# Other places for eight token tiles and eight modulation rows in the first pass of an attention and mixer kernel

## The chip, the cores and the metric

One core of a Trainium2 chip runs the whole kernel. The metric is the device time of one execution in microseconds (us); a kernel's time is the median of several executions. The engines are PE (TensorE matmul; PEld are its weight loads), DVE (VectorE), ACT (ScalarE), POOL (GpSimd) and SP (SyncE), whose queue issues the transfers.

## What is computed

A block with modulated layer norms: infini-attention with a compressive memory (32 heads of width 32, 4 segments of 512 tokens), then a token-mixing MLP. All tensors are float32.

```python
mod = (silu(c) @ w_mod).reshape(1, 6, 1, -1)
sa, ca, ga, sb, cb, gb = (mod[:, i] for i in range(6))
h = layernorm(x) * (1 + ca) + sa               # x: 1 x 2048 x 1024
x = x + ga * A(h)                              # A: attention, below
h = layernorm(x) * (1 + cb) + sb
x = x + gb * B(h)                              # B: gelu(W1 h^T) W2 over the tokens

# A, for segment s in 0..3 of each head; M and z start at 0
p = softmax(qs @ ks.T * scale + causal mask)
o = g * (phi(qs) @ M) / (phi(qs) @ z + 1e-6) + (1 - g) * (p @ vs)
M, z = M + phi(ks).T @ vs, z + sum(phi(ks))
```

The projections are h @ wq, h @ wk, h @ wv, and the outputs of all heads go through wo.

## The kernel before

**Precision.** Most matmuls run on operands that are split into a high part (rounded to the matmul's format) and a low part (the rest): three matmuls high x high, high x low and low x high stand for one. The helper split (L117) makes such a pair: a cast on one engine (L121 on ACT or L123) and a subtraction on another (L124). That is done for weights, for the normalised tokens and for the scores' operands.

**Two passes.** The attention works on 16 iterations t in each of two passes (its, L364): pass 0 treats segments 0 and 1 for the eight groups of four heads, pass 1 segments 2 and 3. Pass 0 converts each group's weights: fetch_part (L150) loads 128 x 1024 of them into a buffer "raw", split_part (L155) makes two pairs of it (two casts L121 on ACT, two subtractions L124 on DVE), and keep_w (L172) stores the pairs in DRAM (wsp), from where pass 1 loads them. There are three parts for each group.

**The loop.** The loop at L690 goes over steps n from -3. Step n issues the scores of head n (scores, L512: matmuls a, three exponentials on ACT, a cast L532 on ACT and two subtractions L534 on POOL), the row maxima of head n + 3 (maxima, L473: matmuls sx, sy, sz into two PSUM banks, each taken by DVE at L485), the values of head n - 1 (values, L536) and a piece of the projections of head n + 8 (project, L380: matmuls nps at L194, kps, qps at L202, and the transfers sk at L376 to L378 that lay out the operands of the next heads). A step number thus counts heads; head n belongs to iteration n // 4.

**Work planned into steps.** plan (L594) hangs a function on a step, later (L662) a fetch on one step and its use on another. The functions of a step are issued at its end (L715). With "V", "A" or "G" each instruction of the function on that engine is queued behind a mark of the same step (behind, L504): the last row maximum on DVE, which in step n is that of head n + 3 (L485), the cast of head n on ACT (L532), or its subtraction on POOL (L534). Apart from that an instruction goes into its engine's queue at the place that the builder's schedule gives it, from the order of issue and from when its inputs and buffers are free. Each engine then works through its queue in order; so does SP with its transfers.

**Token tiles.** Segments 2 and 3 are tokens 1024 to 2047, eight tiles of 128. load_gaw (L668) loads one tile of x into gaw, a single buffer. token_tile (L254) normalises it in place (statistics L129 to L137 and L240 on DVE with two small ACT steps, then L241 on ACT), transposes it in eight blocks on PE into PSUM (L262), applies the modulation on the way back (eight ACT steps at L265), casts the high part into a raw buffer (L268 on ACT), subtracts for the low part (two POOL steps at L270), and stores both in DRAM (hT1, L273). reload_h (L359) brings them back for pass 1. Before, tile i is loaded in step 6i and treated in step 6i + 3.

**Late modulation.** The rows 2048 to 6143 of the transposed w_mod are needed late. mod_fetch (L571) loads 128 of them into a raw buffer, mod_late (L576) multiplies them by the activated c and sums each row on DVE (L577). After row 7 and after row 31 mod_rows (L584) transposes the sums and stores them. Row j is fetched in step 36 + 2j, for j from 8 on in step 44 + 2j, and summed one step later.

**The buffers raw.** There are three. The weight parts, the high parts of the token tiles, the modulation rows and later the parts of wo share them, in program order.

**The plan of the weights.** Group g (2 to 7) starts at n = 8g - 13: parts are fetched in steps n, n + 1 and n + 2 and converted in n + 1, n + 3 and n + 4. That gives conversions in steps 4, 6, 7, then 12, 14, 15, then 20, 22, 23, and so on to 44, 46, 47.

Of the kernel before, what the change touches and what calls it, by code (L numbers as in the profile page):

```python
# [31 lines left out]
VL = 1  # L32
PHB = 2
P32B = 2
ML0 = 36
HB = 3
WO0 = 65
WOS = 6
# [5 lines left out]
def attention_and_mlp(ctx, tc, x, wq, wkv, wo, beta, w1, b1, w2, b2, c, wm_a, wm_b, out):  # L44
    nc = tc.nc
    V, A, G, T, SY = nc.vector, nc.scalar, nc.gpsimd, nc.tensor, nc.sync
# [27 lines left out]
    def bank(tag, bufs, name):  # L74
        return psum.tile([P, 512], F32, tag=tag, bufs=bufs, name=name)
# [162 lines left out]
    def norm_x(pool, t):  # L238
        mv = ln_stats(pool, t, "a")
        V.tensor_scalar(mv[:, 3:4], mv[:, 0:1], -1.0, mv[:, 2:3], op0=ALU.mult, op1=ALU.mult)  # L240
        A.activation(t, t, AF.Identity, scale=mv[:, 2:3], bias=mv[:, 3:4])  # L241
# [12 lines left out]
    def token_tile(tt):  # L254

        r = gaw
        norm_x(a, r)
        for half in range(2):
            ps = bank("s2", 2, f"hpl{tt}_{half}")
            for i in range(4):  # L260
                ct = 4 * half + i
                T.transpose(ps[:, 128 * i:128 * i + 128], r[:, P * ct:P * ct + P], ident)  # L262
            for i in range(4):
                ct = 4 * half + i
                A.activation(r[:, P * ct:P * ct + P], ps[:, 128 * i:128 * i + 128], AF.Identity,  # L265
                             scale=saca[:, ct, 1:2], bias=saca[:, ct, 0:1])
        hi = a.tile([P, D], F32, tag="raw", bufs=3, name=f"hix{tt}")
        A.copy(hi.bitcast(F32R), r)  # L268
        for c in (slice(0, 512), slice(512, 1024)):
            G.tensor_tensor(r[:, c].bitcast(F32R), r[:, c], hi[:, c], op=ALU.subtract)  # L270
        i = tt % 4
        for part, t in enumerate((hi, r)):
            SY.dma_start(hT1[tt // 4 - 2, :, :, part, P * i:P * i + P].rearrange("k p n -> p k n"),  # L273
                         t.rearrange("p (k n) -> p k n", k=NK))
# [296 lines left out]
    def mod_fetch(j):  # L571
        r = a.tile([P, D], F32, tag="raw", bufs=3, name=f"rawm{j}")
        SY.dma_start(r, wm_b[P * j:P * j + P])
        return r

    def mod_late(j, r):  # L576
        V.scalar_tensor_tensor(r, r, 1.0, scb, op0=ALU.mult, op1=ALU.mult, accum_out=mcol[:, j:j + 1])  # L577
        if j == 7:
            mod_rows(0, 8)
        if j == 31:  # L580
            V.tensor_scalar_add(mcol[:, 16:24], mcol[:, 16:24], 1.0)
            mod_rows(8, 32)
# [11 lines left out]
    def plan(n, f, engines=""):  # L594
        todo.setdefault(n, []).append((f, engines))
# [66 lines left out]
    def later(n, fetch, m, f, engines):  # L662

        got = []
        plan(n, lambda: got.append(fetch()))
        plan(m, lambda: f(got[0]), engines)

    def load_gaw(i):  # L668
        with tc.issue_after(last_sk[0, 3].ins):
            return SY.dma_start(gaw, x[P * (8 + i):P * (9 + i)])  # L670

    for i in range(8):
        later(6 * i, lambda i=i: load_gaw(i),
              6 * i + 3, lambda r, i=i: token_tile(8 + i), "V")
    for g in range(2, NG):
        n = 8 * g - 13
        plan(n, lambda g=g: W.__setitem__((0, g), {}))
# [2 lines left out]
                  n + n1, lambda r, g=g, kind=kind, part=part: split_part(g, kind, part, r), "A")  # L680
        plan(n + 4, lambda g=g: keep_w(g))
    for j in range(32):
        n = ML0 + 2 * j + (8 if j >= 8 else 0)
        later(n, lambda j=j: mod_fetch(j), n + 1, lambda r, j=j: mod_late(j, r), "V")
    plan(WO0 - 3, lambda: spread(gaw, 0))
    for i in range(8):
        n = WO0 + WOS * i
        later(n, lambda i=i: wo_fetch(i), n + 1, lambda r, i=i: wo_split(i, r), "G")

    for n in range(-LEADS, 4 * NI + VL):  # L690
# [18 lines left out]
        if 4 * NI - 5 <= m < 4 * NI + 3:  # L709
            i = m - 4 * NI + 5  # L710
# [434 lines left out]
```

## Time and profile before

| | us |
|---|---|
| median of 3 executions | 2233.55 (2232.91 to 2235.92) |
| profiled execution | 2234.21 |
| its span, first to last instruction | 2231.4 |
| mean granted clock of PE | 0.995 |
| DVE busy in the span | 1675.0 |
| ACT busy in the span | 1137.5 |

How to read the rows. The profile is one execution. L194 is line 194 of the kernel. "nps<-wv,h" names the tile written and the tiles read. In a timeline row stand the start, the duration, engine, line, operation, tiles and count, and in brackets the idle time of the engine just before it and what ended that. In a row of groups stand the busy time and the mean ns of one after the bar, then the idle time before them with its releasers. In the rows of one tile's instructions stand the shortest, the median and the longest duration in ns, and the first and the last start. "SPq" is the issue of a transfer, not the transfer. A busy PE is not a PE at its peak: the granted clock says at what share of full speed its clock ran.

### The profile page before, as it was taken

How to read it: one execution, taken by the hardware profiler on the slowest of the kernel's cores; microseconds unless marked ns; L12 is line 12 of the kernel's file. 1: busy time of each engine (PE TensorE's matmuls, PEld its weight loads, DVE VectorE, ACT ScalarE, POOL GpSimd, SP SyncE). 2: the span in 40 equal slices, each digit the busy share in tenths (PEclk: the TensorE clock that was granted, in tenths of full speed). 3: DMA queues.
4: the chain of work that ended last, by engine and by line, in shares of the span. 5: the costliest groups of instructions: out<-in, count | busy, mean ns of one | idle time of the engine just before them, and what ended most of it. 6: DMA issues, size and time to landing. Idle time of an engine off the chain costs nothing.

```text
span 2231.4 us, 38273 instructions
## 1 busy us (share of the span) xinstructions
PE 2195.2 (98%) x13786; PEld 1886.7 (85%) x13786; DVE 1675.0 (75%) x3762; ACT 1137.5 (51%) x2082; POOL 725.4 (33%) x831
## 2 busy tenths in 40 slices
PE   8999999999999999999999999999999999999999
PEld 5989898889989999988888888888888888888887
DVE  7677676767776776765858766888888886969687
ACT  5477776667666666654636533533334242424232
POOL 2175665656766766653001200033330000000000
PEclk9999999999999999999999999999999999999999
DMA  7657565688556666764654587655556542414134
GB/s 284 190 168 210 161 186 156 186 287 245 158 178 192 189 192 202 216 217 151 217 198 177 222 314 268 245 221 221 206 204 224 208 142 63 150 57 146 57 123 151
DMA packets 175185, 423.05 MB, mean 190 GB/s; under 512 B 17524, under 2 KB 71828, under 8 KB 166036
## 3 DMA queue, kind: packets, MB, share of 16 engines
q1 hardware_dynamic: 174996, 420.61, 57.2%
q8 instruction: 109, 1.79, 0.3%
q14 instruction: 80, 0.66, 0.1%
HBM read 244.62 MB, written 125.06 MB: 166 GB/s over the span
## 4 chain that ended last, share of the span: by engine, by line
PE 87%; DVE 4%; POOL 3%; DMA 3%; ACT 3%; issue 1%; SPq 1%; ACTq 0%; POOLq 0%; DVEq 0%
PE mx L925 47%; PE nps L194 12%; PE po L795 7%; PE qps L202 7%; PE pv L548 3%; POOL ph L534 2%; PE a L519 1%; PE sz L483 1%; PE sx L483 1%; DMA rawm<-in_wm_b_dram 1%; PE a L522 1%; PE rd L455 1%; PE sy L483 1%; PE up L465 1%; PE srow L296 1%
## 5 line engine op out<-in xcount | busy, mean ns | idle before, releaser
L925 PE MATMUL mx<-bU,sp 128*128 128x512 f32 x2352 | 534.4, 389 | 1.0 <-DVE ac L932 0.9
L925 PEld LDWEIGHTS mx<-bU,sp 128*128 128x128 f32 x2352 | 441.3, 188 | 93.6 <-issue 1.3
L121 ACT CAST sp<-wr 128x384 fp32r<-128x384 f32 (+2 forms) x408 | 217.2, 545 | 432.6 <-PE mx L925 351.9
L534 POOL TENSOR_TENSOR ph<-p,ph 128x640 f16<-128x640 f32 x256 | 384.9, 1524 | 161.2 <-ACT ph L532 156.9
L194 PE MATMUL nps<-wv,h 128*128 128x256 f32 x3072 | 435.2, 282 | 1.7 <-DVE h L124 0.7
L925 PE MATMUL mx<-bA,sp 128*128 128x512 f32 x1764 | 430.5, 389 | 0.0
L194 PEld LDWEIGHTS nps<-wv,h 128*128 128x128 f32 x3072 | 403.4, 189 | 9.7 <-DVE h L124 2.0
L925 PEld LDWEIGHTS mx<-bA,sp 128*128 128x128 f32 x1764 | 331.2, 188 | 68.7
L124 DVE TENSOR_TENSOR sp<-wr,sp 128x384 fp32r<-128x384 f32 (+2 forms) x408 | 259.7, 647 | 25.4 <-ACT sp L121 25.2
L932 DVE TENSOR_TENSOR ac<-mx,ac 128x512 f32<-128x512 f32 x280 | 189.9, 687 | 85.9 <-PE mx L925 85.5
L202 PE MATMUL qps<-h,wq 128*128 128x512 f32 x768 | 197.2, 400 | 0.4
L532 ACT CAST ph<-p 128x1280 f16<-128x1280 f32 x128 | 161.0, 1259 | 39.5 <-POOL p L530 39.1
L795 PE MATMUL po<-wo,ots 128*128 128x512 f32 x768 | 180.0, 390 | 0.0
L795 PEld LDWEIGHTS po<-wo,ots 128*128 128x128 f32 x768 | 143.5, 188 | 28.9
L202 PEld LDWEIGHTS qps<-h,wq 128*128 128x128 f32 x768 | 142.0, 191 | 28.7 <-ACT vp L406 1.2
L925 PE MATMUL mx<-bB,sp 128*128 128x512 f32 x588 | 164.0, 389 | 0.0
L530 POOL TENSOR_SCALAR_AFFINE_SELECT p<-p 128x256 f32<-128x256 f32 x256 | 123.1, 491 | 91.8 <-ACT p L527 50.9
L548 PE MATMUL pv<-vp,ph 128*128 128x97 bf16 (+1 forms) x2560 | 142.7, 202 | 0.7 <-DVE red L555 0.4
L548 PEld LDWEIGHTS <-ph 128*128 128x128 f16 x2560 | 115.8, 98 | 21.8 <-issue 9.3
L925 PEld LDWEIGHTS mx<-bB,sp 128*128 128x128 f32 x588 | 110.4, 188 | 22.9
L485 DVE CUSTOM_DVE_ANT_0 sx<-sx,mask 128x128 f32<-128x128 f32 (+1 forms) x256 | 93.8, 366 | 47.5 <-PE sx L483 45.2
L932 DVE TENSOR_TENSOR cc<-mx,cc 128x512 f32<-128x512 f32 x140 | 94.9, 684 | 36.7 <-PE mx L925 36.7
(207 smaller groups left out, 3146.6 us busy)
## 6 DMA issues: line engine op xcount, KB each, us to landing
sk<-sg SPq DMA_DIRECT2D x384, 128.0 KB
wr<-in_w_dram SPq DMA_DIRECT2D x28, 1024.0 KB
wr<-in_w_dram SPq DMA_DIRECT2D x32, 768.0 KB
bstu<-ucd SPq DMA_DIRECT2D x28, 768.0 KB
wsp<-wv SPq DMA_DIRECT2D x32, 512.0 KB
rawm<-in_wm_b_dram SPq DMA_DIRECT2D x32, 512.0 KB
wv<-wsp SPq DMA_DIRECT2D x32, 512.0 KB
pcd<-cc SPq DMA_DIRECT2D x14, 1024.0 KB
```

The costliest lines, as they stand in the source:

```text
L121: last_hi[0] = A.copy(hi, src)
L124: return lo_eng.tensor_tensor(lo, src, hi.bitcast(F32), op=ALU.subtract)
L194: T.matmul(ps[:, aa], h[:, j, 128 * tt:128 * tt + 128], wt[:, i, o:o + 256], start=(n == 0), stop=(n >= 6 * NK - 2), skip_group_check=True)
L202: T.matmul(ps, wt[:, i, o:o + 128], h[:, j], start=(k + n == 0), stop=(3 * k + n == 3 * NK - 1))
L485: marks[4 * t + h - LEADS, "V"] = V.tensor_tensor_reduce(o, o, mask[:, 384 - 128 * i:], 1.0, -3.0e38, op0=ALU.add, op1=ALU.max, accum_out= ...
L530: G.affine_select(w, w, pattern=[[0, 2], [1, 128]], compare_op=ALU.is_ge, fill=0.0, base=0, channel_multiplier=-1)
L532: marks[n, "A"] = A.copy(ph[:, 0], p32)
L534: marks[n, "G"] = G.tensor_tensor(ph[:, 1, c], p32[:, c], ph[:, 0, c], op=ALU.subtract)
L548: T.matmul(pv[:, i, 0:w], ph[:, part, o:o + 128], d["vp"][:, j, h, 0:w], start=(n == 0), stop=(n == 19), skip_group_check=True)
L795: T.matmul(ps, os_[:, i, P * ct:P * ct + P], wop[ct, nh][:, j], start=(n == 0), stop=(n == 3 * NK - 1))
L925: T.matmul(ps, ops[q][:, i, P * k:P * k + P], b[:, j], start=(m == 0 and first), stop=(m == 3 * nk - 1), skip_group_check=True)
L932: V.tensor_tensor(d, ps, d, op=ALU.add)
```

## The change

Token tile i is loaded and treated in other steps, with two steps between load and treatment instead of three: treated in 2, 8, 11, 16, 19, 24, 27 and 32 instead of 3, 9, 15, 21, 27, 33, 39 and 45. The modulation rows 0 to 7 are fetched in steps 33, 34, 40, 41, 42, 48, 49 and 50 instead of 36, 38, 40, 42, 44, 46, 48 and 50, and summed one step after their fetch as before. The rows from 8 on stay in their steps (44 + 2j, written in another way). The weights keep their plan.

```diff
-ML0 = 36
+ML0 = 44
...
-    for i in range(8):
-        later(6 * i, lambda i=i: load_gaw(i),
-              6 * i + 3, lambda r, i=i: token_tile(8 + i), "V")
+    for i, n in enumerate((2, 8, 11, 16, 19, 24, 27, 32)):
+        later(n - 2, lambda i=i: load_gaw(i), n, lambda r, i=i: token_tile(8 + i), "V")
...
     for j in range(32):
-        n = ML0 + 2 * j + (8 if j >= 8 else 0)
+        n = (33, 34, 40, 41, 42, 48, 49, 50)[j] if j < 8 else ML0 + 2 * j
         later(n, lambda j=j: mod_fetch(j), n + 1, lambda r, j=j: mod_late(j, r), "V")
```

## The prediction

> **What bounds the kernel now.** I read the page first, then the busy time of each engine by stretches, then the waits of TensorE (PE), then the timeline at each hole.
>
> ```profile
> span 2231.4 us, 38273 instructions
> PE 2195.2 (98%) x13786; PEld 1886.7 (85%) x13786; DVE 1675.0 (75%) x3762; ACT 1137.5 (51%) x2082; POOL 725.4 (33%) x831
> ```
>
> PE is busy for 98% of the span, so no edit that leaves its work as it is can bring more than the 36.2 us in which it is idle. The stretches below (columns: length, then busy us of PE, PEld, DVE, ACT, POOL, then granted clock, DMA share, GB/s) say where these lie.
>
> ```profile
> 75.00:340.00 265.00, 260.43 (x2241) 238.41 (x2240) 190.67 (x561) 186.90 (x357) 153.19 (x181) 0.97 0.60 173
> 340.00:475.00 135.00, 123.64 (x1050) 112.28 (x1049) 100.11 (x284) 92.59 (x173) 81.49 (x89) 0.97 0.67 197
> 500.00:960.00 460.00, 456.27 (x4104) 419.25 (x4103) 332.54 (x1013) 296.98 (x526) 319.18 (x380) 1.00 0.64 194
> 960.00:2231.00 1271.00, 1266.03 (x5787) 1048.10 (x5785) 985.22 (x1767) 509.72 (x937) 143.84 (x117) 1.00 0.52 183
> PE sz L483 <- DVE mx L485: 8.4, 4, 4.0
> ```
>
> The first pass of the attention runs from about 75 to 475. Its last 135 us lose 11.4 us of PE, the 265 us before them 4.6, and the whole second pass 3.7. The last row is from the waits within 340 to 475: 8.4 of the 11.4 us are four waits of one kind. PE wants to write the next score tile, and the bank is still held because DVE has not taken the row maximum of the one before. DVE is not short of time there (100 of 135 us); it works through its queue in order, and something long stands ahead of the maximum. The timeline says what:
>
> ```profile
> 358.93 0.42 SPq L573 DMA_DIRECT2D rawm<-in_wm_b_dram  x1
> 367.99 1.47 DVE L577 SCALAR_TENSOR_TENSOR rawm<-rawm,scb 128x1024 f32<-128x1024 f32 x1 [5.36 <-DMA rawm<-in_wm_b_dram]
> 370.31 0.79 PE L483 MATMUL sz<-sk 96*128 96x512 f32 x1 [3.99 <-DVE mx L485]
> 392.61 0.95 DVE L124 TENSOR_TENSOR wq<-rawq,wq 128x512 fp32r<-128x512 f32 x1
> 394.40 0.49 PE L483 MATMUL sz<-sk 96*128 96x512 f32 x1 [2.04 <-DVE mx L485]
> 430.11 1.30 DVE L577 SCALAR_TENSOR_TENSOR rawm<-rawm,scb 128x1024 f32<-128x1024 f32 x1
> 432.61 3.21 DVE L124 TENSOR_TENSOR wv<-rawv,wv 128x512 fp32r<-128x512 f32 x2
> 436.65 0.50 PE L483 MATMUL sz<-sk 96*128 96x512 f32 x1 [1.62 <-DVE mx L485]
> ```
>
> At 358.93 the first modulation row is fetched; it lands 9.06 us later, DVE has stood 5.36 us for it, and PE 3.99 us behind DVE. At 394 and 436 the maxima stand behind the second halves of a weight conversion (L124), with token-tile or modulation work of the same queue around it. The clock adds to this:
>
> ```profile
> 365.00:370.00 5.00, 1.32 (x23) 1.02 (x20) 2.01 (x5) 4.38 (x9) 3.56 (x5) 0.92 0.47 114
> 370.00:375.00 5.00, 4.20 (x24) 3.41 (x24) 4.96 (x18) 0.58 (x1) 1.43 (x3) 0.50 0.56 198
> 375.00:380.00 5.00, 5.00 (x23) 4.15 (x21) 2.21 (x3) 3.17 (x5) 2.08 (x2) 0.89 0.83 274
> 245.00:250.00 5.00, 2.46 (x21) 1.79 (x17) 5.00 (x12) 5.00 (x12) 3.91 (x5) 0.98 0.45 182
> 250.00:255.00 5.00, 5.00 (x38) 4.46 (x38) 3.19 (x11) 3.78 (x7) 2.77 (x2) 0.68 0.31 91
> 120.00:125.00 5.00, 4.52 (x38) 3.01 (x34) 4.74 (x20) 5.00 (x11) 2.40 (x5) 0.85 0.32 66
> 125.00:130.00 5.00, 4.84 (x26) 3.71 (x24) 3.43 (x10) 3.24 (x7) 5.00 (x7) 0.50 0.81 239
> 130.00:135.00 5.00, 5.00 (x18) 4.16 (x17) 2.73 (x4) 4.69 (x7) 2.53 (x4) 0.63 1.00 264
> ```
>
> After the hole at 366 the granted clock is 0.50 from 370 to 375 and 0.89 to 380: 5 x 0.50 + 5 x 0.11 = 3.05 us of full-speed work lost. The hole at 245 (2.54 us idle) is followed by 0.68: 1.6 us more. Between 120 and 135, with little idle time but few matmuls, the clock costs 0.75 + 2.5 + 1.85 = 5.1 us. So a stall is dearer than its idle time.
>
> The Trainium skill (TensorE: Matmul & The Clock Gate, What's actually happening) says that the array falls to half rate after an idle window of about 3.4 us and needs a busy one to rise again. By that rule a hole of 4 us is followed by half clock, some 1.7 us a window (an estimate from the page's window), and holes of 1 to 2 us cost their idle time only; the trace agrees at 366 and disagrees at 245 and 120, where the single holes are shorter and the clock falls all the same. By the rule the sum below would be -9.0 instead of -9.6 us, and the slower rival would end at no change, since four meetings at 2.54 us are 10.2 us against credits of 6.2 + 2.45 + 1.62.
>
> **The change, part by part.** No instruction and no transfer is added or removed: eight token tiles and eight modulation rows move, each with all that it issues.
>
> ```profile
> L265 ACT ACTIVATE gaw<-hpl,saca x64: 443/470/519, 119.4 to 448.8; 128x128 f32<-128x128 f32 x64
> L129 DVE BATCH_NORM_STATS2 st<-gaw x16: 673/680/690, 109.2 to 429.5; 128x6 f32<-128x512 f32 x16
> L270 POOL TENSOR_TENSOR gaw<-gaw,hix x16: 1281/1286/2268, 126.3 to 452.1; 128x512 fp32r<-128x512 f32 x16
> L241 ACT ACTIVATE gaw<-gaw,mv x8: 1232/1244/1247, 114.4 to 441.6; 128x1024 f32<-128x1024 f32 x8
> L268 ACT CAST hix<-gaw x8: 1039/1052/1115, 123.9 to 449.7; 128x1024 fp32r<-128x1024 f32 x8
> L577 DVE SCALAR_TENSOR_TENSOR rawm<-rawm,scb x32: 1201/1277/2374, 368.0 to 877.5; 128x1024 f32<-128x1024 f32 x32
> ```
>
> One tile is 8 x 0.47 + 1.24 + 1.05 = 6.1 us of ACT, 2 x 0.68 us and a few small operations of DVE, 2.6 us of POOL, eight short PE transposes, one load and two stores on SP's queue. A modulation row is one load and 1.28 us of DVE. The old plan spread the tiles over steps 3 to 45, the new one ends at 32; the two tiles that leave the steps after 33 (12.2 us of ACT) come into a stretch where ACT has 265.0 - 186.9 = 78 us free. In sum that is nothing on PE; what counts is where each lands.
>
> *Modulation rows.* Rows 0 and 1 go to steps 34 and 35, ahead of the conversions of 36, 38, 39; rows 2 to 4 to 41 to 43, between 39 and 44; rows 5 to 7 to 49 to 51, behind 47. Their buffers ("raw", three, also used by each weight part and by a token tile's high part) are handed out in program order, so their fetch is now asked for once tile 32's high part has its buffer, before the weight parts of 35 and 36 instead of behind them. I credit the removal of the hole at 366: 4.48 us idle (5 - 1.32 + 5 - 4.20) + 3.05 of clock = **7.5**. If the rows are late again, this is 0.
>
> *The tiles of 39 and 45* leave. The holes at 394 (2.04, with 0.41 just before) and at 436 (1.62) lie where tile, modulation and conversion met in DVE's queue; only the conversion stays, and the modulation rows now stand clear of 39 and 44. Credit **2.45 + 1.62**; none if the conversion alone makes them. What is late next at 455 to 470 (steps 46 and 47, modulation rows 5 to 7 still close behind) I leave as it is.
>
> *The tiles before 33.* The one of step 21 met the conversion of step 20:
>
> ```profile
> 244.94 1.48 DVE L124 TENSOR_TENSOR wv<-rawv,wv 128x512 fp32r<-128x512 f32 x1 [1.58 <-ACT wv L121]
> 247.09 0.65 PE L262 MATMUL hpl<-ident,gaw 128*128 128x128 f32 x4 [1.21 <-ACT gaw L241]
> 249.07 0.50 PE L483 MATMUL sz<-sk 96*128 96x512 f32 x1 [1.33 <-DVE mx L485]
> ```
>
> PE stood for the tile's ACT step and then for a maximum behind the conversion: 2.54 + 1.6 of clock = 4.1 us. It moves to step 19; I credit half, **2.1**, since its buffer may make it late. The buffer gaw is single:
>
> ```profile
> 341.61 1.24 ACT L241 ACTIVATE gaw<-gaw,mv 128x1024 f32<-128x1024 f32 x1
> 354.64 0.51 SPq L273 DMA_DIRECT2D hT<-gaw  x1
> 358.50 0.37 SPq L670 DMA_DIRECT2D gaw<-in_x_dram  x1
> L485 DVE CUSTOM_DVE_ANT_0 sz<-sz,mask 128x512 f32<-128x512 f32 x19 | 13.2, 696 | 4.6 <-PE sz L483 4.6
> ```
>
> From a tile's first ACT step to its last store 13.0 us, to the next load 16.9; with a landing like the 9.06 us above (as a bound) the next tile can begin after some 26 us. The pairs 8/11, 16/19 and 24/27 leave three steps; the last row counts 19 heads in the 135 us from 340 to 475, 7.1 us a step, so 21 us. The second of a pair may slide by about one step, into 12, 20 or 28, where conversions are.
>
> There is a second lag. A tile is queued behind the maxima of step n, which are those of head n + 3; a conversion behind the copy of head n itself:
>
> ```profile
> L485 DVE CUSTOM_DVE_ANT_0 sz<-sz,mask 128x512 f32<-128x512 f32 x12 | 8.5, 707 | 7.5 <-PE sz L483 7.4
> 126.58 0.73 DVE L485 CUSTOM_DVE_ANT_0 sz<-sz,mask 128x512 f32<-128x512 f32 x1
> 132.95 1.15 ACT L121 CAST wv<-rawv 128x512 fp32r<-128x512 f32 x2
> ```
>
> The first row counts twelve last maxima (sz) from 60 to 127.3, so the one at 126.58 is head 11's and frees tile 8; the conversion of step 4 begins only at 132.95. So a tile "between" 7 and 12 can run among the conversions of 4, 6 and 7. I charge one such meeting at the price of the one at 245: **+4.1**; bounds 0 and four of them (tiles 8, 16, 24, 32), 16.6. For the low end stands
>
> ```profile
> 200.00:225.00 25.00, 24.89 (x220) 22.98 (x219) 18.55 (x50) 21.02 (x42) 16.72 (x22) 1.00 0.80 235
> ```
>
> a stretch in which the tile of step 15 ran among the conversions of 14 and 15 and PE lost 0.11 us. I take one, nearer to this row, because most meetings cost nothing. The 5.1 us at 120 to 135 I leave: the first tile's ACT work moves out ahead by one head, but tile 8 comes in behind; bounds 5.1 less and 5.1 more.
>
> Sum: -7.5 - 2.45 - 1.62 - 2.1 + 4.1 = -9.6 us. The profiled execution took 2234.2 us (2.8 around its span), 0.7 over the median of 2233.55; 2234.2 - 9.6 = 2224.6, and the forecast is **2225**, its own range 2219 to 2229.
>
> **The rivals.** *Slower: the maxima meet the conversions in the first half.* By the lag of three heads, tiles 8, 16, 24 and 32, each right behind two conversions, run among them; DVE's queue is in order, and PE waits at each. Price 4.1 each: +16.6 - 11.6 (the three first credits, the fourth not earned) = +5.0, so 2239. It decides from the third meeting on (12.4 against 11.6). For it: 126.58 ahead of 132.95. Against it: 200 to 225. Chance 0.26.
>
> *No change that can be told: the late rows stay late or the gain is given back.* The fetch still has one step (7.1 us) to land and needed 9.06; if the hole at 366 only moves, 2.45 + 1.62 + 2.1 - 4.1 = 2.1 stay, so 2232. This is also the case in which the change doesn't do what it says: places in the program are only lower bounds, the single gaw and the three raw buffers set the time. For it: the landing. Against it: the burst of two weight parts, gaw and row at 357 to 359 is pulled apart. Chance 0.20.
>
> *More than forecast:* the sparse stretch at 120 to 135 keeps its clock as well, -9.6 - 5.1 = -14.7, so 2219.5. For it: ACT is busy 5.00 of 5.00 there with the tile. Against it: DVE is at 4.74 with four heads of maxima, which stay. Chance 0.12. The forecast itself has 0.42.
>
> **How the numbers follow.** About 0.2%, 4.5 us, is what a measurement of this kernel can tell from none. Faster than 2229 are the forecast and the last rival, 0.42 + 0.12 = 0.54; within, 0.20; slower, 0.26. The range runs from below the last rival, 2216, to a little beyond the slower one's time, 2241; five meetings would pass it.
>
> **What would show it.** Right: no wait of L577 on its transfer over 2 us before 450; PE busy over 131 of the 135 us from 340 to 475; granted clock 1.00 there; the last L270 before about 360. Half of the credit at 245 right: no PE wait on L241 above 1 us. Wrong: more than 10 us of PE lost between 75 and 340, new waits of sz on maxima there, or half clock at the places of tiles 8, 16, 24 or 32. A changed time of the second pass or the mixer would show a mechanism that I have not named.

## The result, and the profile after

| | before | after |
|---|---|---|
| median | 2233.23 (2231.22 to 2235.92, 4 executions) | 2258.66 (2254.67 to 2259.65, 4 executions) |
| profiled execution, its span | 2231.4 | 2256.2 |
| mean granted clock | 0.995 | 0.990 |

The ratio is 1.0108, 95% interval 1.0095 to 1.0122: slower by 25.4 us between the medians and by 24 us by the ratio, where 2225 was forecast and 2241 was the upper end of the range. In the table of experiments below, the medians of "after, reloads held" and "after, weights held" leave out one execution of over 5000 us each.

The page of after, its span and busy times:

```profile
span 2256.2 us, 38264 instructions
PE 2205.6 (98%) x13786; PEld 1890.8 (84%) x13786; DVE 1668.3 (74%) x3762; ACT 1134.0 (50%) x2082; POOL 721.1 (32%) x831
```

PE has the same 13786 matmuls. Of the 24.8 us in span, 10.4 are longer busy time (2205.6 - 2195.2, matmuls at a lower clock) and 14.4 more idle time. The stretches of after (columns as in the prediction):

```profile
75.00:340.00 265.00, 251.19 (x2091) 226.69 (x2090) 179.85 (x542) 183.17 (x355) 144.19 (x168) 0.97 0.60 174
340.00:475.00 135.00, 133.47 (x1215) 122.04 (x1215) 108.34 (x289) 94.58 (x173) 93.56 (x104) 1.00 0.67 200
475.00:530.00 55.00, 47.33 (x391) 42.33 (x390) 27.28 (x89) 27.90 (x49) 23.82 (x31) 0.88 0.70 210
530.00:960.00 430.00, 422.05 (x3763) 387.94 (x3760) 302.79 (x928) 269.13 (x481) 283.97 (x342) 0.99 0.62 190
960.00:1100.00 140.00, 136.97 (x894) 114.96 (x893) 76.66 (x224) 70.18 (x121) 60.31 (x71) 0.99 0.56 179
```

And the last three of before, cut in the same places:

```profile
475.00:530.00 55.00, 54.60 (x503) 50.76 (x502) 31.80 (x101) 33.16 (x61) 31.04 (x40) 1.00 0.81 263
530.00:960.00 430.00, 426.67 (x3841) 391.88 (x3840) 311.15 (x939) 276.08 (x489) 299.46 (x355) 1.00 0.64 191
960.00:1100.00 140.00, 139.16 (x820) 115.98 (x819) 92.03 (x241) 74.02 (x132) 44.87 (x53) 1.00 0.60 198
```

Read them from the top. Up to 340, PE loses 13.8 us instead of 4.6. From 340 to 475 it loses 1.5 instead of 11.4, and the clock is 1.00. So far this is a draw. From 475 to 530, where the second pass begins and where nothing was edited, it loses 7.7 us instead of 0.4 and runs at 0.88. Behind that, up to 1100, it loses 11.0 instead of 4.2.

Fixed stretches mix the loss with the shift that it makes. A second reading avoids that: the matmuls of each trace are counted at the median spacing that their shape has in the trace of before, and for a given amount of this work the moment is taken at which PE starts it, after minus before. This is the **lag**. In after it is 16.3 us where before stands at 343, 0.6 at 475, 13.1 at 524, 14.9 at 892 and 24.0 at the end. So the first pass, in which all the edits lie, nets to nothing: it loses 16 us and wins them back. The 24 us come in two pieces: **12.5 at the change of passes and 10.9 in the second pass**.

### The change of passes

The timeline of PE in after (the number in brackets is the idle time just before, with its releaser), and the busy time in steps of 5 us:

```profile
502.83 0.80 PE L483 MATMUL sx<-sk 96*128 96x128 f32 x2 [5.26 <-DMA sk<-sg]
507.76 0.77 PE L483 MATMUL sx<-sk 96*128 96x128 f32 x2 [1.36 <-DMA sk<-sg]
```

```profile
495.00:500.00 5.00, 2.00 (x15) 1.23 (x14) 2.58 (x13) 2.61 (x4) 3.52 (x4) 0.96 1.02 276
500.00:505.00 5.00, 1.70 (x8) 1.28 (x8) 1.33 (x6) 1.26 (x2) 0.00 (x0) 0.50 0.94 253
505.00:510.00 5.00, 3.64 (x18) 2.86 (x18) 3.17 (x11) 1.49 (x4) 4.02 (x5) 0.50 0.47 154
510.00:515.00 5.00, 5.00 (x30) 4.19 (x29) 1.79 (x5) 3.58 (x6) 2.41 (x2) 0.68 0.29 116
```

PE waits 5.26 and then 1.36 us for the operands of the next heads. Idle time plus busy time x (1 - clock) is 3.1 + 4.2 + 3.2 + 1.6 = 12.0 us, nearly the step of the lag (12.5). Why the operands are late stands in SP's queue, first that of after, then that of before (start, duration of the issue, line, tiles):

```profile
491.45 0.52 SPq L361 DMA_DIRECT2D h<-hT  x1
492.01 0.45 SPq L573 DMA_DIRECT2D rawm<-in_wm_b_dram  x1
492.57 0.38 SPq L169 DMA_DIRECT2D wv<-wsp  x1
493.04 0.63 SPq L376 DMA_DIRECT2D sk<-sg  x1
493.73 0.61 SPq L377 DMA_DIRECT2D sk<-sg  x1
494.39 0.59 SPq L378 DMA_DIRECT2D sk<-sg  x1
495.08 0.81 SPq L590 DMA_DIRECT2D modd<-mrow  x1
496.00 0.35 SPq L169 DMA_DIRECT2D wv<-wsp  x1
496.44 0.45 SPq L169 DMA_DIRECT2D wq<-wsp  x1
```

```profile
472.67 7.08 SPq L361 DMA_DIRECT2D h<-hT  x8
480.71 0.69 SPq L376 DMA_DIRECT2D sk<-sg  x1
...
498.40 0.59 SPq L378 DMA_DIRECT2D sk<-sg  x1
499.09 0.43 SPq L590 DMA_DIRECT2D modd<-mrow  x1
499.63 0.35 SPq L169 DMA_DIRECT2D wv<-wsp  x1
```

In before the twelve sk transfers of heads 56 to 59 are asked for with no load among them (only one store and four small nt transfers), and the weights of the second pass (wv, 512 KB each, as are h and rawm) come behind them. In after a token tile, a modulation row and a weight part, 1.5 MB together, stand right ahead of three of those sk transfers (128 KB each). The last of the three is asked for at 494.39, and PE can go on at 502.83: 8.4 us, with the transfer engines at 1.02 and 0.94 of their time. The three of the next head are asked for from 501.18 on, behind two more weight parts, and PE waits the 1.36 us for them. No transfer was added; the order in the queue is another. Large loads ahead are not enough by themselves: in before eight token tiles, 4 MB, stand ahead of all twelve (the first row), but the first head's three are asked for by 485.96 and its sx runs at 494.21, without a wait.

### The second pass

One row of DVE and two of PE, from the timelines of after, and the clock behind the first:

```profile
879.47 1.42 DVE L577 SCALAR_TENSOR_TENSOR rawm<-rawm,scb 128x1024 f32<-128x1024 f32 x1 [3.93 <-DMA rawm<-in_wm_b_dram]
881.93 0.80 PE L483 MATMUL sz<-sk 96*128 96x512 f32 x1 [1.68 <-DVE mx L485]
941.05 0.45 PE L522 MATMUL a<-sk 98*128 98x384 f32 x1 [1.21 <-ACT p L527]
```

```profile
880.00:885.00 5.00, 3.32 (x10) 2.50 (x9) 5.00 (x17) 2.76 (x4) 2.31 (x5) 0.69 0.38 140
```

The first two rows are the hole at 366 of the kernel before over again, in another place: a modulation row is late, DVE stands 3.93 us for it, the maximum behind it is late, PE stands 1.68 us, and the clock falls. The third is one of several short waits of other kinds. Before has no wait of PE over 0.7 us between 475 and 1100.

### The profile page after: what moved, and what is told of

Read it like the earlier page. It is cut to its first block, busy times and chain, and to the rows that moved or that the text cites. A ratio compares the mean times of both kernels' runs of the same rounds, so it can differ in the third digit from the quotient of the medians.

```text
span 2256.2 us, 38264 instructions
## 1 busy us (share of the span) xinstructions
PE 2205.6 (98%) x13786; PEld 1890.8 (84%) x13786; DVE 1668.3 (74%) x3762; ACT 1134.0 (50%) x2082; POOL 721.1 (32%) x831
## 4 chain that ended last, share of the span: by engine, by line
PE 81%; DVE 5%; DMA 5%; ACT 4%; POOL 3%; issue 2%; SPq 1%; ACTq 0%; DVEq 0%; POOLq 0%
PE mx L924 47%; PE nps L194 11%; PE po L794 6%; PE qps L202 6%; PE pv L548 3%; POOL ph L534 2%; DMA sk<-sg 1%; ACT ph L532 1%; PE sx L483 1%; PE a L519 1%; PE sz L483 1%; PE rd L455 1%; DVE wv L124 1%; PE up L465 1%; PE srow L296 1%
## 5 line engine op out<-in xcount | busy, mean ns | idle before, releaser
L534 POOL TENSOR_TENSOR ph<-p,ph 128x640 f16<-128x640 f32 x256 | 377.6, 1496 | 151.5 <-ACT ph L532 149.8
L520 ACT ACTIVATE p<-a,shift 128x512 f32<-128x512 f32 x128 | 88.1, 689 | 75.2 <-PE a L519 48.9
```

Source lines behind the costliest of these rows:

```text
L534: marks[n, "G"] = G.tensor_tensor(ph[:, 1, c], p32[:, c], ph[:, 0, c], op=ALU.subtract)
```

## The experiments

"Lag" below is the measure just explained, read where before stands at 343, 475 and 524 us and at the end. Lags are those of the profiled execution, which lies up to 5 us from its median. Each ratio is to the kernel before on the same chip.

| kernel | median | ratio [95%] | lag 343 | 475 | 524 | end |
|---|---|---|---|---|---|---|
| after | 2258.66 | 1.0108 [1.0095, 1.0122] | 16.3 | 0.6 | 13.1 | 24.0 |
| rows alone | 2233.32 | 0.9986 [0.9976, 0.9997] | -1.3 | -4.4 | -2.4 | 2.0 |
| tiles alone | 2259.98 | 1.0102 [1.0084, 1.0120] | 16.0 | 11.4 | 16.6 | 25.8 |
| tiles evenly | 2234.79 | 1.0000 [0.9990, 1.0011] | 13.9 | -1.7 | -2.4 | 1.7 |
| last two tiles late | 2252.06 | 1.0068 [1.0051, 1.0085] | 9.2 | 9.0 | 10.5 | 18.9 |
| after, reloads held | 2244.96 | 1.0045 [1.0028, 1.0061] | 17.0 | 1.3 | 4.3 | 9.5 |
| after, weights held | 2253.98 | 1.0083 [1.0066, 1.0100] | 16.3 | 0.6 | 10.1 | 20.7 |
| after, both held | 2247.34 | 1.0047 [1.0032, 1.0062] | 17.1 | 1.7 | 1.9 | 13.0 |
| before, reloads held | 2238.86 | 1.0023 [1.0013, 1.0032] | -0.1 | 2.0 | 1.4 | 3.0 |
| before, tile 39 to 40 | 2222.47 | 0.9947 [0.9930, 0.9963] | -4.4 | -10.6 | -10.2 | -14.3 |
| before, row 2 later | 2231.92 | 0.9985 [0.9975, 0.9994] | -1.6 | 0.2 | 0.2 | -3.1 |
| rows, and 39 to 40 | 2237.21 | 1.0007 [0.9998, 1.0017] | -0.2 | -3.1 | -1.8 | 4.4 |
| after, 27 to 28 | 2248.37 | 1.0049 [1.0034, 1.0064] | 12.9 | 0.8 | 8.5 | 15.1 |
| after, 32 to 31 | 2238.44 | 1.0014 [1.0003, 1.0026] | 14.9 | 1.5 | 2.0 | 4.1 |
| after, 27 to 26 | 2263.91 | 1.0134 [1.0111, 1.0157] | 21.0 | 7.9 | 19.0 | 29.0 |
| after, 11 to 12 | 2237.40 | 1.0011 [1.0000, 1.0021] | 11.0 | -2.2 | -0.4 | 5.6 |
| after, row 30 summed later | 2247.44 | 1.0065 [1.0047, 1.0084] | 18.2 | 2.5 | 12.6 | 18.5 |
| both held, row 30 later | 2239.37 | 1.0020 [1.0006, 1.0034] | 17.3 | 1.6 | 2.0 | 9.7 |

### The two parts alone, and other places

**The rows alone**, the tiles where they were:

```diff
-ML0 = 36
+ML0 = 44
...
-        n = ML0 + 2 * j + (8 if j >= 8 else 0)
+        n = (33, 34, 40, 41, 42, 48, 49, 50)[j] if j < 8 else ML0 + 2 * j
```

> The eight modulation rows in their new steps, the token tiles in their old ones. Theory D (density: eight tiles in the steps 2 to 32 hold up the first half, the rows' new places are a gain): PE loses as before between 75 and 340 (4 to 6 us), the hole of 4.5 us at 366 is gone, the time is 2222 to 2230. Theory R (reshuffle: any edit lets the builder order all that follows anew, and what the change of passes and the second pass lose is decided by that): PE loses more than 8 us between 475 and 960, against 3.7 before, and the time is 2230 to 2245.

**The tiles alone**, the rows where they were:

```diff
-    for i in range(8):
-        later(6 * i, lambda i=i: load_gaw(i),
-              6 * i + 3, lambda r, i=i: token_tile(8 + i), "V")
+    for i, n in enumerate((2, 8, 11, 16, 19, 24, 27, 32)):
+        later(n - 2, lambda i=i: load_gaw(i), n, lambda r, i=i: token_tile(8 + i), "V")
```

> The token tiles in their new steps, the modulation rows in their old ones. Theory D: PE loses 12 to 15 us between 75 and 340 as in the changed kernel, and the two tiles that left the steps after 33 give back 5 to 10 us after 340; the time is 2238 to 2250, and what is lost after 475 is as little as before. Theory R: the loss between 475 and 960 is again over 8 us, and the time 2250 or more.

The slowdown is in the tiles, the rows alone are slightly faster. By the time and by what is lost from 475 to 960 (8.9 us with the rows alone, 16.6 with the tiles alone) both runs came out as theory R. Between 343 and 475 the rows alone win 3.1 us of lag, the tiles alone 4.6, both together 15.7: the parts are not additive. With either of them left, other holes stay in that stretch (PE busy 128.6 with the rows alone, 130.2 with the tiles alone, 133.5 with both).

**The changed kernel with its tiles at even distances:**

```diff
-    for i, n in enumerate((2, 8, 11, 16, 19, 24, 27, 32)):
+    for i, n in enumerate((2, 6, 10, 15, 19, 23, 28, 32)):
```

> The changed kernel with the same eight tiles at an even pace over the same steps (2, 6, 10, 15, 19, 23, 28, 32), so that none waits for the single buffer behind the one before, and five of them in steps that convert weights. Theory D: the first half loses the same 12 to 15 us between 75 and 340. Rival B (the single buffer and the pairs three steps apart make the loss): the first half loses 5 to 8 us. Rival C (meetings with conversions make the loss): it loses more than 15 us.

Its first two rows of stretches:

```profile
75.00:340.00 265.00, 249.45 (x2099) 225.88 (x2098) 178.84 (x539) 185.54 (x355) 143.70 (x169) 0.97 0.60 172
340.00:475.00 135.00, 134.83 (x1229) 124.43 (x1228) 108.58 (x293) 94.50 (x176) 92.54 (x104) 1.00 0.70 210
```

It loses even more up to 340 (15.6 us) and wins it all back, and then nothing happens at the change of passes: 2234.79, no difference. So eight tiles before 33 are not what costs 24 us, and since no two of these stand three steps apart, the pairs are not what costs 16 in the first half. Whether meetings with conversions cost it (rival C) stays open: 15.6 us of idle time lies just inside its range, but the lag at 343 is 13.9, below the 16.3 of the changed kernel.

**The changed kernel with its last two tiles at 40 and 45:**

```diff
-    for i, n in enumerate((2, 8, 11, 16, 19, 24, 27, 32)):
+    for i, n in enumerate((2, 8, 11, 16, 19, 24, 40, 45)):
```

> The changed kernel with its last two tiles at 40 and 45 instead of 27 and 32, so that the first half has six tiles, in the pairs of the change. Density theory (each tile more in the first half costs there, wherever it stands): 75 to 340 loses 3 to 8 us instead of 13.8, and 340 to 475 loses 4 or more. Meeting theory (pairs three steps apart and tiles behind two conversions cost): 75 to 340 still loses 10 or more, since three pairs and tiles 8, 16 and 24 are still there. Time 2225 to 2240 by the first theory, 2240 or more by the second.

```profile
75.00:340.00 265.00, 252.85 (x2147) 229.18 (x2146) 180.66 (x542) 184.26 (x352) 147.56 (x173) 0.97 0.59 171
340.00:475.00 135.00, 126.18 (x1100) 114.61 (x1099) 96.58 (x276) 87.85 (x166) 81.77 (x92) 0.97 0.62 183
```

The first half loses 12.2 us with six tiles, so the loss there isn't simply the number of tiles: the theory that each tile costs wherever it stands is refuted in that form (and the other, the pairs, by the even tiles above). What the lag shows is finer. With the same places up to tile 24, this kernel lags 9.1 at 311 and after 9.8. From there to 343 after adds 6.5 with its last two tiles and this one 0.1; from 343 to 475 after wins 15.7 and this one 0.2. So the last two tiles cost 6.5 us early and some 15 late: moving those two early is worth 9 us. The 9 us that are lost by 311 belong to the new order of the first six, and where exactly is not settled: they are spread over many short waits (below).

### The queue at the change of passes

**The changed kernel with the reloads of the tokens of segment 2 held** until the sk transfers of heads 56 to 59 have been asked for (reload_h in the function that plans the second pass), and the same edit in the kernel before:

```diff
-                if seg == 3:
-                    s.enter_context(tc.issue_after((last_sk[15, 3] if ct < 4 else last_nt[14, 3]).ins))
+                s.enter_context(tc.issue_after((last_sk[14, 3] if seg == 2 else
+                                                last_sk[15, 3] if ct < 4 else last_nt[14, 3]).ins))
```

> The changed kernel with one edit at the change of passes: the eight loads of segment 2's tokens (reload_h) are queued behind the last transfer sk of iteration 14. Theory Q (in the changed kernel five transfers of 512 KB were queued ahead of sk transfers of iteration 14, and PE stands for these): PE loses under 2.5 us between 475 and 530 instead of 7.7, the clock stays at 1.00 there, and the time is 2240 to 2250 against 2258. Rival O (the order on PE costs it, since the transposes kps and the products qps of iteration 15 stand behind four heads of maxima, whatever the transfers do): PE still loses over 5 us there and the time stays 2254 to 2262.

> The kernel before with the edit of after_reload2. Theory Q: nothing to gain there (PE lost 0.4 us between 475 and 530): 2230 to 2240, a few us lost if the pages now come late for iteration 16. If it gains over 5 us, the transfers also held up the kernel before at a place that its PE rows do not show.

**The changed kernel with the first weight loads of the second pass held** behind the same transfers, and then with both kinds held:

```diff
-                with tc.issue_after(last_sk[t - 2 if t > 16 else 0, 3].ins):
+                with tc.issue_after(last_sk[t - 2, 3].ins):
```

> The changed kernel with the first weight loads of pass 1 (wv, wq from wsp) queued behind the last sk transfer of iteration 14; the last load of segment 2 and modulation row 10 stay ahead of two of its heads. Theory Q: part of the hole goes, PE loses 2 to 5 us between 475 and 530, the time is 2246 to 2256. Rival O: over 5 us lost, 2254 to 2262.

> The changed kernel with both kinds of loads of the change of passes held behind the sk transfers of heads 56 to 59 (token reloads of segment 2, first weight loads of the second pass). If the loss at the change of passes is the queue alone: PE loses under 2.5 of 55 us from 475 to 530 and the clock is at least 0.96. If holding moves the burst behind the next heads: a loss of 4 or more, with half clock, as with the weights held alone. What is left against the kernel before is then the second pass: 2243 to 2252 by the first, 2252 to 2260 by the second.

The stretch from 475 to 530, first with both held, then with the weights alone:

```profile
475.00:530.00 55.00, 54.67 (x500) 50.96 (x499) 35.07 (x113) 33.66 (x62) 29.53 (x39) 1.00 0.81 259
```

```profile
475.00:530.00 55.00, 49.08 (x420) 45.02 (x418) 27.52 (x92) 27.94 (x49) 23.86 (x31) 0.91 0.76 239
```

With both held the change of passes costs 0.3 us of idle time at clock 1.00, and the lag moves from 1.7 to 1.9 instead of from 0.6 to 13.1. With the reloads alone held 3.0 us remain. There the first weight loads, which weren't held, come behind all twelve sk as well, so this doesn't tell the two kinds apart. With the weights alone held 9.5 remain, and PE loses 5.9 of 55 us where 2 to 5 were expected: a token tile and a modulation row still stand ahead of six of the sk (PE waits 3.05 us for sk at 500.33), and the nt transfers now come behind three weight loads (2.68 us at 505.58). In the kernel before, where the queue was in order, the same edit brings nothing (slower by 0.2%). The 12.5 us are thus put down to the queue. The holds also make PE's own order anew, from somewhere between 470 and 480 us on, so rival O isn't excluded by them alone; what speaks for the queue is that PE's long waits there end with the late transfers, in after, with the weights held and in two kernels below. But with both held the time is 2247, not 2235: 11 us still arise in the second pass.

**The changed kernel with one tile a step later** (27 becomes 28), by which all twelve sk transfers come ahead of the weights:

```diff
-    for i, n in enumerate((2, 8, 11, 16, 19, 24, 27, 32)):
+    for i, n in enumerate((2, 8, 11, 16, 19, 24, 28, 32)):
```

> The changed kernel with one tile one step later (27 becomes 28). Its order of issue puts all twelve sk transfers of heads 56 to 59 behind h2_5 and ahead of wv, where the changed kernel has h2_7, row 10 and three 512 KB weight loads among them. Theory Q (the loss at the change of passes is sk transfers queued behind the weight loads): PE busy from 475 to 530 at least 52 of 55 us, no sx wait on sk over 2 us there, time 2233 to 2248. Rival P (the places of the tiles themselves cost the time, through the first half): loss from 475 to 530 stays near 7.7 us and the time within 4 us of 2258. Both: 75 to 340 loses 12 to 16 us, 340 to 475 under 3.

```profile
504.03 0.77 PE L519 MATMUL a<-sk 98*128 98x512 f32 x1 [5.05 <-DMA sk<-nt]
```

```profile
494.95 0.85 SPq L361 DMA_DIRECT2D h<-hT  x2
495.85 0.43 SPq L573 DMA_DIRECT2D rawm<-in_wm_b_dram  x1
496.37 0.38 SPq L169 DMA_DIRECT2D wv<-wsp  x1
496.85 2.63 SPq L498 DMA_DIRECT2D sk<-nt  x4
```

This was half a miss, and an instructive one. The wait of sx on the sk transfers is gone, as forecast, and the time is only 0.4 above its range. But PE loses 5.1 of 55 us all the same, where at most 3 were expected: now the four small transfers of 2 KB from nt (L498, the row maxima for the scores) are asked for behind four loads of 512 KB, and PE waits 5.05 us for those. Any transfer that the scores need can be the one behind the loads.

### One step's move, and what the order of issue does

All these kernels have the same instructions. For each engine the program's instructions were listed in the order of issue (some 8700 rows for PE, equal neighbours in one), and two lists compared row by row from the end. Families agree to the end of the program, from a place between 500 and 690 us on:

```
                                       last rows of PE   which begin   lag from 524
                                       that are equal    at about      to the end
before; tile 39 to 40; row 2 later          3937            686        0, -4.1, -3.3
rows alone; rows and 39 to 40; 11 to 12     4916            566        4.4, 6.2, 6.0
27 to 28; after with reloads held           4838            585        6.6, 5.2
tiles evenly; 32 to 31                      5448            510        4.1, 2.1
tiles alone; after with both held           4310            655        9.2, 11.1
after; 27 to 26                             5323            535        10.9, 10.0
```

Kernels with one order agree within 4 us in the second pass, though their first passes differ in all ways; between the orders lie up to 15 us. Each of these lags is of one execution, and single executions of one order can differ by almost 5 us (last section), so a few us between two rows of the table prove nothing. That was a reading of runs already made, so it was tried on three that were not, each a single tile moved by a single step in the changed kernel:

```diff
-    for i, n in enumerate((2, 8, 11, 16, 19, 24, 27, 32)):
+    for i, n in enumerate((2, 8, 11, 16, 19, 24, 27, 31)):
```

> The changed kernel with its last tile one step earlier (32 becomes 31). From the change of passes on (the last 5448 rows of PE's queue) the order of issue is word for word that of the kernel with even tiles, and SP's queue holds the sk transfers of heads 56 to 59 together. Order theory (what comes after 475 is decided by the order alone): PE loses 2.5 us or less from 475 to 530, and behind it at most 3 us more than the kernel before, as the even one did; with a first pass like that of the changed kernel 2232 to 2241. Place theory (these places of tiles cost it, however the rest is ordered): within 4 us of 2258.

```diff
-    for i, n in enumerate((2, 8, 11, 16, 19, 24, 27, 32)):
+    for i, n in enumerate((2, 8, 11, 16, 19, 24, 26, 32)):
```

> The changed kernel with one tile one step earlier (27 becomes 26), a move of the same size. From the change of passes on (the last 5323 rows of PE's queue) the order is word for word that of the changed kernel, with the same weight loads among the sk transfers of heads 56 to 59. Order theory: PE waits on sk at 500 to 510 as there, 6 to 9 us lost from 475 to 530, 9 to 13 us more behind it; 2253 to 2262. Rival (a step's move makes it better whatever the order): 2248 or less.

```diff
-    for i, n in enumerate((2, 8, 11, 16, 19, 24, 27, 32)):
+    for i, n in enumerate((2, 8, 12, 16, 19, 24, 27, 32)):
```

> The changed kernel with one tile one step later (11 becomes 12). The last 4916 rows of PE's queue are word for word those of the kernel with the new rows alone, which is slower by some 6 us than the kernel before in the second pass, and the sk transfers of heads 56 to 59 stand together. Order theory: at most 3 us lost from 475 to 530, 4 to 8 us behind it; 2237 to 2247. Place theory: within 4 us of 2258.

2238.44, 2263.91 and 2237.40: they fall apart by 26 us as the order said, though the move is equally small. The one with the order of the changed kernel is above its range by 2 us, from a first pass that is worse by 7 (lag 7.9 at 475); behind 524 it adds the 10.0 that were expected, and the others 2.1 and 6.0. From 475 to 530 of 32 to 31, and the wait of sx on the sk transfers in 27 to 26:

```profile
475.00:530.00 55.00, 54.28 (x501) 49.78 (x500) 34.45 (x114) 33.26 (x61) 28.62 (x39) 1.00 0.80 252
```

```profile
509.77 0.80 PE L483 MATMUL sx<-sk 96*128 96x128 f32 x2 [4.89 <-DMA sk<-sg]
```

Three more are moves of one step in the kernel before. **One tile from 39 to 40, one row by a step, and the first of these with the new rows:**

```diff
-    for i in range(8):
-        later(6 * i, lambda i=i: load_gaw(i),
-              6 * i + 3, lambda r, i=i: token_tile(8 + i), "V")
+    for i, n in enumerate((3, 9, 15, 21, 27, 33, 40, 45)):
+        later(n - 3, lambda i=i: load_gaw(i), n, lambda r, i=i: token_tile(8 + i), "V")
```

> The kernel before with one token tile moved by one step, from 39 to 40; nothing else. Theory D: 2231 to 2236, nothing that can be told. Theory R: all that follows step 39 is ordered anew, so that the second pass (475 to 960) loses 3 to 15 us and the time moves by more than 5 us.

> The kernel before with one modulation row (row 2) fetched and summed one step later, 41 and 42 instead of 40 and 41; a second sample of what a small edit does by ordering the rest anew. Theory R: the time moves by 3 to 13 us either way, and the lag against the kernel before appears at places after step 41 that the row doesn't touch, the second pass among them. Theory D: 2231 to 2240.

> The kernel before with the new rows of the change and one tile at 40 instead of 39: the two edits that were faster alone (by 2.5 and 12 us). If both gains come from the same holes (366 to 440), they don't add: 2220 to 2230, PE loses under 5 us from 340 to 475, and the second pass decides the rest. If they add: under 2220. If the order made anew goes against it: 2230 or more, with new waits at the change of passes or in the second pass.

The first beats both kernels: 2222.47, ratio 0.9947 [0.9930, 0.9963]. Its time moved by more than 5 us, as theory R had it, but not by a worse second pass, as that theory had it too. The row moved by a step gave 2231.92, inside the range of theory D. It keeps the second pass of the kernel before and fills part of the holes behind 366:

```profile
340.00:475.00 135.00, 130.00 (x1134) 118.97 (x1133) 100.98 (x284) 94.77 (x179) 80.83 (x93) 0.97 0.75 228
```

(4.4 us of its lag at 343 lie ahead of the edit, where its clock didn't fall at 123; the profiled execution, at 2218.9, is 3.6 faster than the median.) With the new rows added the gain is gone, 2237: the two don't add up to 2220 because rows and tile together have the second pass of the rows alone, and a worse 340 to 475 (127.5 us busy) than the move alone.

### One late row in the second pass

**Row 30 of the late modulation summed one step later**, its fetch unmoved, in the changed kernel and in the one with both kinds held. All three orders looked at (PE, SP, DVE) are unchanged up to that sum:

```diff
-        later(n, lambda j=j: mod_fetch(j), n + 1, lambda r, j=j: mod_late(j, r), "V")
+        later(n, lambda j=j: mod_fetch(j), n + 1 + (j == 30), lambda r, j=j: mod_late(j, r), "V")
```

> The changed kernel with row 30 of the late modulation summed one step later (its fetch stays). All orders are word for word those of the changed kernel up to that sum, at 879 us, which then stands behind the next last maximum instead of ahead of it. Theory (the late row stands at the head of DVE's queue for 3.93 us and PE waits 1.68 us for the maximum behind it, with half clock after it): no wait of sz of 1 us or more between 875 and 890, granted clock 1.00 there, 3 to 5 us less lost by 890; 2251 to 2257 unless the order behind it costs or gains more. Rival (the wait is made by something else that is late there): PE waits 1 us or more at the same place.

> The same edit in the kernel with both kinds of loads held, where the row's wait was 4.33 us and PE's behind it 3.10. Theory: that wait of sz between 865 and 880 is gone and 3 to 6 us less are lost by 880; 2240 to 2246 unless the order behind it costs or gains more. Rival: PE waits 1 us or more at the same place, 2245 or more.

The same five microseconds as above in the first of them:

```profile
880.00:885.00 5.00, 5.00 (x24) 4.11 (x23) 4.83 (x10) 2.54 (x4) 3.55 (x5) 1.00 0.44 151
```

The row is summed at 881.79 without a wait, PE doesn't stand for sz there, and the clock stays at 1.00. Between 855 and 892 the lag grows by 0.5 us instead of 3.0, a gain of 2.5 where 3 to 5 were expected; with both kinds held by 0.0 instead of 4.2. So this meeting is worth 2.5 to 4.2 of the 11 us. Both medians came out lower than the ranges, 2247.44 and 2239.37; the rest is the order behind the sum, which was made anew here too and has other waits, so it proves nothing more. The remaining 6 to 8 us of the second pass were not taken apart one by one.

## Why the prediction was wrong

**The credits of the second half were right, and too small.** "The removal of the hole at 366" came as described: the row is fetched at 355.0 and waited for 0.32 us instead of 5.36, and the waits of sz fall from 8.4 to 1.1 us from 340 to 475 of after:

```profile
359.89 1.22 DVE L577 SCALAR_TENSOR_TENSOR rawm<-rawm,scb 128x1024 f32<-128x1024 f32 x1 [0.32 <-DMA rawm<-in_wm_b_dram]
PE sz L483 <- DVE mx L485: 1.1, 1, 1.1
```

PE is busy 133.47 of 135 us (over 131 was the mark) at clock 1.00. The credits there were 7.5 + 2.45 + 1.62 = 11.6; the lag fell by 15.7. (The 7.5 takes 1 - clock times whole windows; with the busy time in them it is 7.2. The 5.1 at 120 to 135 is 4.95 in the same way.) What the sum didn't see is that rows and tiles had to go together (3.1 and 4.6 alone).

**The credit at 245 was right and was taken back 20 us later.** The lag falls by 3.8 us between 239 and 256 of before, nearly the whole 4.1 of which 2.1 were credited, and rises by 5.5 from there to 268. The stretches of after show both, the old place at full clock and the new one:

```profile
245.00:250.00 5.00, 5.00 (x58) 4.92 (x58) 2.60 (x11) 2.40 (x3) 1.65 (x3) 1.00 0.37 77
265.00:270.00 5.00, 3.32 (x32) 2.65 (x32) 4.59 (x12) 3.46 (x6) 2.07 (x4) 1.00 0.32 82
270.00:275.00 5.00, 4.36 (x31) 4.17 (x28) 3.82 (x15) 2.92 (x6) 3.80 (x5) 0.66 0.90 206
```

**"The tiles before 33" was mis-sized: +4.1 charged, 16.3 measured** (lag at 343). The sign of being wrong that was named for it, more than 10 us of PE lost between 75 and 340, came true with 13.8. The rival "the maxima meet the conversions in the first half" had nearly the size, 16.6, but not the mechanism, and its chance of 0.26 for a slower kernel fits the direction by luck: the waits of sz there are 1.7 us, against 1.5 before. Three of the 14 kinds of wait of after from 75 to 340:

```profile
PE sx L483 <- DMA sk<-sg: 2.6, 3, 1.1
PE a L525 <- ACT p L520: 2.1, 3, 0.8
PE sz L483 <- DVE mx L485: 1.7, 4, 1.0
```

These are many waits of less than 1.2 us on ACT, on DVE and on transfers, and the charge had looked for one meeting of one kind. By itself this error would have changed little: with the 15.7 it leaves the lag at 0.6, and the time at no change.

**The step that failed is the one that isn't in the sum: nothing was charged for what comes after 475.** The prediction began its parts with "No instruction and no transfer is added or removed" and let the second pass stand, with its 3.7 us of idle time. It also said that places in the program are only lower bounds, and the text ahead of it that a queue follows the builder's schedule, but this was used for one rival inside the first pass only. The runs put 23.4 us there: 12.5 because loads of 512 KB (tokens, a modulation row, weights) came to stand among the transfers of heads 56 to 59 (0.2 when tokens and weights are held), and 10.9 in a second pass whose order was made anew (0 to -4 in the kernels that keep the order of before, 1.6 to 11 in all others, of which those under 5 are no clearer than two executions of one order). That one step's move of one tile switches both on or off shows that they belong to the order and not to the places of the tiles. The last mark of the prediction, "a changed time of the second pass or the mixer would show a mechanism that I have not named", is what came true.

Not shown is why nearly every new order of the second pass looks worse than that of the kernel before. One meeting of it was taken away and gave about what it should (2.5 and 4.2 us); for the others there are only the waits in the trace.

## What to carry to other kernels

Where a builder makes the queues from estimated times, an edit of places is an edit of every queue behind it: before a stretch is costed at nothing, compare the order of issue of both programs, above all the few transfers that the next operands hang on and what stands ahead of them. A gain in the edited stretch and the time of the whole are then two questions, and one step's move of any part is the cheapest test of whether a result belongs to the idea or to the order that it happened to get. Loads that nobody needs for a while are worth an explicit hold behind the transfers that somebody needs now, where the order isn't fixed otherwise.

## What the runs showed that was not expected

In two places here a small transfer was as late as the large ones ahead of it. 128 KB asked for at 494.39 behind 1.5 MB let PE go on 8.4 us later; four transfers of 2 KB, asked for from 496.85 on behind 2 MB, 7.2 us later. In both the transfer engines' share is about 1 in the 5 us before.

The clock falls after short holes as well, again against the rule that the prediction took from the Trainium skill (TensorE: Matmul & The Clock Gate, What's actually happening), by which an idle window of about 3.4 us is needed. After the single wait of 1.68 us at 881.93 the clock of the five microseconds around it is 0.69, and without that wait it is 1.00, in the kernel that sums this row a step later and whose order is the same up to there; after three waits of 0.75, 0.93 and 0.64 us at 268 to 271 it is 0.66.

One order of issue isn't one time. The two kernels with both kinds held have the same order of PE, SP and DVE up to 870, and their lags where before stands at 818 differ by 4.9 us (0.0 and 4.9), from a wait of 2.96 us at 535 in one of them and what follows it. Differences of less than that between two profiled executions say nothing here; the medians do.
